# Early q, k and v loads over 128 partitions, 64x64 turns of q and k, a layer norm without a reciprocal, and a new order

## The chip, the cores and the metric

One core of one Trainium2 chip runs the whole kernel. The metric is the device time of one execution in microseconds. The core's engines are named as the profile names them: PE (matrix products, with PEld for its weight loads), DVE (vector), ACT (scalar), POOL (GpSimd) and SP, which only issues transfers. Every transfer of this kernel is issued by SP, in program order, into one queue that is served by the core's 16 DMA engines.

## The reference, cut to what matters

```python
# q, k, v: (8 batches, 8 heads, 576 positions, 64), float32
q_d, k_d, v_d = means over groups of 4 positions          # 144 pooled positions
out_d  = softmax(q_d @ k_d.T / 8) @ v_d                   # dense attention on the pooled rows
out_up = repeat(out_d, 4 positions)
scores = where(|i - j| < 4, q @ k.T / 8, -1e9)            # a band of 7 positions
x      = out_up + softmax(scores) @ v                     # 4608 tokens x 512
h      = x @ w_in                                         # 512 -> 1024 (weights arrive as float64)
solu   = h * softmax(h)
ln     = (solu - mean(solu)) / sqrt(var(solu) + 1e-6) * g_ln
out    = ln @ w_out                                       # 1024 -> 512
```

## The kernel before

The work has two halves that run interleaved. **Attention** goes batch by batch (8 of them). For a batch, q and k are loaded in four pairs of heads, turned so that the head dimension lies on partitions (`qT`, `kT`), and summed over groups of four into `qd` and `kd`. The pooled part (`Pooled`, two groups of pairs) makes scores `sd`, the softmax `pd`, its transpose `pdt`/`pdT` and the product `po` with the pooled values `vd`. The local part works on windows of 64 positions: scores `sc`, softmax `pl`, transpose `plt`/`plT`, and the product `xp` with `vw`, another load of v. Both are added into `x`. **The feed-forward half** goes tile by tile, 36 tiles of 128 tokens: `xhl` splits x into a high and a low part, `ffn_in` makes `h` with 24 matmuls of 128x512, then the softmax, `e`, the mean and the variance; `e` is written to memory as `u` and read back as `v` in another layout (`ffn_back`), transposed by 32x32 blocks on DVE, split into `uh` and `ul`, and multiplied by `w_out` in `ffn_out` (`o`, again 24 matmuls), whose result is scaled by `s` on its way out.

At the start the 16 pieces of the two weight matrices are loaded as float64 (512 KB each, tiles `stage` and `w_2` ... `w_15`) and turned into high and low float32 parts, mostly on DVE. Batches 0 and 1 are "early" (`EARLY = 2`): their q and k are loaded in rows and turned on PE against the identity (`qp`, `kp`); later batches are turned on DVE.

`load_vs` loads the values for the pooled sum, three tiles `vs_0` to `vs_2` for each batch, each with four positions side by side in a row of 256 elements. `pooled_vsum` adds them into `vd` (lines L466 and L469 of before, on POOL or DVE). All three must be summed before `po`.

Nothing here is ordered by the hardware's choice: `plan` is a list of steps, the table `ORDER` says in what order the steps are written, and `OTHER` names the steps that go to their second choice of engine. Each engine then runs its own instructions strictly in that order. SP's transfers have eight semaphores in turn (DMAHW0 to DMAHW7), and an issue waits until the one eight before it has landed, so at most eight are in flight.

Of the kernel before, what the change touches and what calls it, by code (L numbers as in the profile page):

```python
# [10 lines left out]
F32 = mybir.dt.float32  # L11
# [117 lines left out]
def pooled_local_attention_then_solu_ffn(  # L129
# [343 lines left out]
    class EarlyBatch(Batch):  # L473

        TT = 6
        TP = S // TT

        def room(self):  # L480
# [625 lines left out]
```

## Time and profile before

| | |
|---|---|
| time, median of 3 runs | 596.7 us (593.45 to 599.17) |
| the profiled execution | 600.77 us, of which the span is 599.0 us |
| mean granted PE clock | 0.975 |
| PE busy | 562.0 us, 94% |
| DVE / ACT / POOL busy | 469.1 / 331.6 / 297.0 us |
| transfers | 101.27 MB, mean 169 GB/s |
| chain that ended last | PE 52%, DVE 16%, SP's queue 10%, DMA 8% |

The page's busy shares are means over a start of some 120 us, in which weights are unpacked and two batches are prepared, a long middle in which attention and the feed-forward tiles alternate on PE, and a short end. The stretches have to be read one by one. A row of the timeline or of a group gives start, busy time, line, engine, operation, output<-input and count.

### The profile page before, as it was taken

To read this page: it belongs to the slowest core of one execution; us is meant where nothing else is said; L and a number is where in the kernel's file an instruction comes from. 1 tells how busy PE (TensorE), PEld (TensorE's weight loads), DVE (VectorE), ACT (ScalarE), POOL (GpSimd) and SP (SyncE) were. 2 spreads that over 40 slices of the span, in tenths; PEclk is the share of its full clock that TensorE was granted. 3 is DMA by queue.
4 is the path that set the end of the run, shared out by engine and by line. 5 is a ranking of instruction groups with operands and counts; after the bars stand their busy time and mean duration, and the time that the engine had idled before them with its cause. 6 is when DMAs were issued, how large, how long until landed. Compare 5 with 4: busy or idle time off the path is not lost.

```text
span 599.0 us, 16898 instructions
## 1 busy us (share of the span) xinstructions
PE 562.0 (94%) x6748; PEld 440.0 (73%) x6748; DVE 469.1 (78%) x712; ACT 331.6 (55%) x692; POOL 297.0 (50%) x444
## 2 busy tenths in 40 slices
PE   7896989899997999999979999999999999999997
PEld 2664757677786778878757778778878788788875
DVE  3989899999986888888868898896898678554551
ACT  2766668655864666536437554547645464443542
POOL 2367388764177464575634446453554464432320
PEclk9989799899997999999999999999999999999999
DMA  8998878579778778776788775678453746133421
GB/s 228 250 202 210 200 154 189 137 180 226 175 160 197 184 181 205 196 139 171 178 182 206 199 229 144 134 164 245 144 142 122 202 119 216 39 106 106 140 89 71
DMA packets 209039, 101.27 MB, mean 169 GB/s; under 512 B 163520, under 2 KB 195264, under 8 KB 208960
## 3 DMA queue, kind: packets, MB, share of 16 engines
q1 hardware_dynamic: 208960, 100.19, 66.4%
q8 instruction: 53, 0.87, 0.6%
q14 instruction: 26, 0.21, 0.1%
HBM read 67.11 MB, written 27.79 MB: 158 GB/s over the span
## 4 chain that ended last, share of the span: by engine, by line
PE 52%; DVE 16%; SPq 10%; DMA 8%; issue 5%; POOL 4%; ACT 2%; DVEq 0%; POOLq 0%; ACTq 0%
PE o L945 21%; PE h L822 20%; SPq L262 4%; DMA v<-u 3%; SPq L693 3%; SPq L897 2%; DMA qm<-in_q_dram 2%; PE warm L1002 2%; PE po L804 2%; DMA stage<-in_moe_w_in_dram 2%; DVE st L831 2%; DVE e L836 2%; DVE w L357 1%; POOL ul L928 1%; PE sd L743 1%
## 5 line engine op out<-in xcount | busy, mean ns | idle before, releaser
L822 PE MATMUL h<-wi_h,xh 128*128 128x512 f32 x288 | 116.5, 405 | 5.5 <-DVE e L836 5.4
L945 PE MATMUL o<-wo_h,uh 128*128 128x512 f32 x288 | 118.0, 410 | 1.0 <-ACT osb L952 0.8
L822 PE MATMUL h<-wi_h,xl 128*128 128x512 f32 x288 | 114.7, 398 | 0.0
L822 PE MATMUL h<-wi_l,xh 128*128 128x512 f32 x288 | 114.7, 398 | 0.0
L945 PE MATMUL o<-wo_l,uh 128*128 128x512 f32 x288 | 113.7, 395 | 0.0
L945 PE MATMUL o<-wo_h,ul 128*128 128x512 f32 x288 | 79.0, 396 | 1.4 <-DVE ul L928 1.4
L822 PEld LDWEIGHTS h<-wi_h,xh 128*128 128x128 f32 x288 | 54.8, 190 | 20.0 <-DVE e L836 4.1
L834 ACT ACTIVATE e<-h,st 128x1024 f32<-128x1024 f32 x36 | 40.1, 1115 | 51.8 <-DVE st L831 50.7
L831 DVE TENSOR_REDUCE st<-h 128x1 f32<-128x1024 f32 x36 | 43.9, 1218 | 29.0 <-PE h L822 27.4
L945 PEld LDWEIGHTS o<-wo_h,uh 128*128 128x128 f32 x288 | 54.3, 189 | 16.6 <-ACT osb L952 2.1
L928 POOL TENSOR_TENSOR ul<-v,uh 128x512 fp32r<-128x512 f32 x39 | 51.3, 1320 | 28.8 <-ACT uh L925 27.3
L945 PEld LDWEIGHTS o<-wo_h,ul 128*128 128x128 f32 x288 | 53.9, 188 | 15.1 <-DVE ul L928 2.2
L925 ACT ACTIVATE uh<-v 128x512 fp32r<-128x512 f32 x70 | 43.2, 625 | 39.2 <-DVE v L918 25.6
L822 PEld LDWEIGHTS h<-wi_h,xl 128*128 128x128 f32 x288 | 54.7, 190 | 13.4 <-POOL xl L979 0.2
L918 DVE STREAM_TRANSPOSE v<-v 128x512 f32<-128x512 f32 x70 | 47.1, 692 | 21.8 <-DMA v<-u 21.2
L822 PEld LDWEIGHTS h<-wi_l,xh 128*128 128x128 f32 x288 | 54.8, 190 | 12.5
L945 PEld LDWEIGHTS o<-wo_l,uh 128*128 128x128 f32 x288 | 54.3, 189 | 11.2
L840 POOL TENSOR_SCALAR st<-st 128x1 f32<-128x1 f32 x36 | 8.8, 244 | 102.3 <-DVE e L836 95.5
L836 DVE SCALAR_TENSOR_TENSOR e<-h,e 128x1024 f32<-128x1024 f32 x36 | 43.7, 1213 | 13.9 <-ACT e L834 13.8
L874 ACT ACTIVATE e<-e 128x1024 f32<-128x1024 f32 x35 | 36.7, 1050 | 16.1 <-DMA u<-e 11.9
L979 POOL TENSOR_TENSOR xl<-x,xh 128x512 fp32r<-128x512 f32 (+1 forms) x29 | 33.7, 1166 | 20.2 <-ACT xh L976 19.9
L952 ACT ACTIVATE osb<-o,s 128x512 f32<-128x512 f32 x36 | 24.4, 678 | 23.1 <-PE o L945 14.5
(127 smaller groups left out, 1099.3 us busy)
## 6 DMA issues: line engine op xcount, KB each, us to landing
u<-e SPq DMA_DIRECT2D x35, 512.0 KB, 3.2
v<-u SPq DMA_DIRECT2D x140, 128.0 KB, 3.3
out_dram<-osb SPq DMA_DIRECT2D x36, 256.0 KB, 3.1
qm<-in_q_dram SPq DMA_DIRECT2D x96, 72.0 KB, 3.3
km<-in_k_dram SPq DMA_DIRECT2D x96, 72.0 KB, 2.4
vs<-in_v_dram SPq DMA_DIRECT2D x24, 256.0 KB, 4.1
vw<-in_v_dram SPq DMA_DIRECT2D x80, 64.0 KB, 3.0
vw<-in_v_dram SPq DMA_DIRECT2D x40, 128.0 KB, 3.4
```

The lines of the kernel that those rows point to most:

```text
L262: nc.sync.dma_start(t[nm][Q * 32:Q * 32 + 32, pr], src[b, 2 * pr + par, :, dh * 32:dh * 32 + 32].rearrange("(k t) d -> t k d", t=32),)
L822: nc.tensor.matmul(hps[:, n, :], src[:, cc, :], wt[:, cc, n * 512:(n + 1) * 512], start=(cc == 0 and src is xh and wt is wi_h), stop=(cc = ...
L831: nc.vector.tensor_reduce(out=nmx, in_=hf, op=ALU.max, axis=AX.X, negate=True)
L834: nc.scalar.activation(e, hf, AF.Exp, bias=nmx, scale=1.0, accum_out=se)
L836: nc.vector.scalar_tensor_tensor(out=e, in0=hf, scalar=1.0, in1=e, op0=ALU.mult, op1=ALU.mult, accum_out=su)
L874: nc.scalar.activation(e0, e, AF.Square, accum_out=m2)
L918: nc.vector.transpose(vg, vg)
L925: nc.scalar.activation(uh, tp, AF.Copy)
L928: (usual if v is None else engine(usual, nc.vector)).tensor_tensor(out=ul, in0=tp, in1=uh.bitcast(F32), op=ALU.subtract)
L945: nc.tensor.matmul(o, src[:, j, :], wt[:, 4 * g + j, :], start=(g == 0 and j == 0 and src is uh and wt is wo_h), stop=(g == 1 and j == 3 a ...
L952: nc.scalar.activation(osb, o, AF.Copy, scale=s)
L979: engine(nc.gpsimd, nc.vector).tensor_tensor(out=l, in0=src, in1=h.bitcast(F32), op=ALU.subtract)
```

## The change

1. **q and k of batches 0 and 1.** A pair of heads was loaded as 96 partitions x 2 heads x 384 elements; it is now 128 partitions x 576 elements, one contiguous run of 2,304 bytes on each. The turn on PE was 12 products of 96x64 by 96x96 for each tensor and pair; it is now 18 products of 64x64 by 64x64.
2. **vs of batches 0 and 1.** A tile was two issues of 64 and 48 partitions x 4 heads x 256 elements; it is now four issues (one for each of four heads `h`) of 128 partitions x 256 elements. The source of each is written as 2 halves x 64 rows x 256 elements. 448 KB a tile become 512 KB.
3. **Layer norm.** The factor was r = 1/se, va = r*r*m2/DFF + 1e-6, s = va^-0.5 * r. It is now s = (m2/DFF + 1e-6*se*se)^-0.5, with se*se*1e-6 made on POOL right behind se. For each tile a DVE reciprocal and two of seven small POOL instructions go.
4. **A new order** of the same steps, and a new list of steps that use their other engine.

```diff
 ORDER = """
-18 21 4 11 23 8 32 22 12 142 143 33 158 34 7 15 159 144 160 145 146 147 148 149 150 151 152 153
...
+9 1 3 4 150 151 152 153 154 155 7 10 2 32 34 142 33 24 158 25 143 156 35 157 36 37 159 26 38 27
...
     def load_vs(b, c):
         vs = big(f"vs_{b}_{c}").rearrange("p (h x) -> p h x", h=H // 2)
-        for half, n in ((0, 64), (1, KN)):
-            src = v[b, half * (H // 2), c * KN * FAC, :]
-            nc.sync.dma_start(
-                vs[half * 64:half * 64 + n],
-                bass.AP(
-                    tensor=src.tensor, offset=src.offset,
-                    ap=[[FAC * D, n], [S * D, H // 2], [1, FAC * D]],
-                ),
-            )
+
+        def source(head, dims):
+            at = v[b, head, c * KN * FAC, :]
+            return bass.AP(tensor=at.tensor, offset=at.offset, ap=[*dims, [1, FAC * D]])
+
+        if b < EARLY:
+            for h in range(H // 2):
+                nc.sync.dma_start(vs[:, h], source(h, [[H // 2 * S * D, 2], [FAC * D, 64]]))
+        else:
+            for half, n in ((0, 64), (1, KN)):
+                nc.sync.dma_start(
+                    vs[half * 64:half * 64 + n],
+                    source(half * (H // 2), [[FAC * D, n], [S * D, H // 2]]),
+                )
         return vs[0:ROOM]
...
         def load_one(self, pr, nm):
-            src = {"q": q, "k": k}[nm]
-            if pr == 3:
-                self.qk[nm, pr] = big(f"{nm}m_{self.b}_3")[:, 0:self.TT * 2 * D]
-            t = self.qk[nm, pr][0:self.TP].rearrange("p (par x) -> p par x", par=2)
-            self.qk[nm, pr] = t.rearrange("p par (t d) -> p par t d", t=self.TT)
             nc.sync.dma_start(
-                t, src[self.b, 2 * pr:2 * pr + 2].rearrange("h (p t) d -> p h (t d)", t=self.TT)
+                self.qk[nm][:, pr * S:(pr + 1) * S],
+                {"q": q, "k": k}[nm][self.b, 2 * pr:2 * pr + 2].rearrange(
+                    "h (p t) d -> (h p) (t d)", t=self.TT
+                ),
             )
...
                 for t in range(self.TT):
-                    at = t % HT * self.TP
                     for par in range(2):
                         nc.tensor.matmul(
-                            tp[rows(par), t // HT, at:at + self.TP],
-                            self.qk[nm, pr][:, par, t],
-                            ident[0:self.TP, 0:self.TP], start=True, stop=True,
+                            tp[rows(par), t], src[rows(par), t], ident[rows(par), rows(par)],
+                            start=True, stop=True,
                         )
...
+        nc.gpsimd.tensor_scalar(
+            out=se, in0=se, scalar1=se, scalar2=1e-6, op0=ALU.mult, op1=ALU.mult
+        )
...
-        nc.vector.reciprocal(out=r, in_=se)
-        yield
-        nc.gpsimd.tensor_tensor(out=va, in0=r, in1=r, op=ALU.mult)
-        yield
         nc.scalar.activation(e0, e, AF.Square, accum_out=m2)
         yield
-        nc.gpsimd.tensor_tensor(out=va, in0=va, in1=m2, op=ALU.mult)
         nc.gpsimd.tensor_scalar(
-            out=va, in0=va, scalar1=1.0 / DFF, scalar2=1e-6, op0=ALU.mult, op1=ALU.add
+            out=m2, in0=m2, scalar1=1.0 / DFF, scalar2=se, op0=ALU.mult, op1=ALU.add
         )
-        nc.gpsimd.tensor_tensor(out=va, in0=va, in1=mhalf, op=ALU.pow)
-        nc.gpsimd.tensor_tensor(out=s, in0=va, in1=r, op=ALU.mult)
+        nc.gpsimd.tensor_tensor(out=s, in0=m2, in1=mhalf, op=ALU.pow)
```

What the order makes of it is seen best in the engines' own sequences. **SP, where the first values are loaded.** In these rows `qm` and `km` are q and k (the numbered names mark the batch's buffer), `vw` and `vs` the two loads of v, `stage` and `w_N` weight pieces; the sizes are partitions x runs x elements. Before, from batch 1's first k load:

```order
L495 DMA km_390<-in_k_dram 96x2x384
L495 DMA km_3_404<-in_k_dram 96x2x384
L495 DMA km_390<-in_k_dram 96x2x384
L337 DMA stage<-in_moe_w_in_dram 128x1024
L495 DMA km_390<-in_k_dram 96x2x384
L294 DMA vs_0_409<-in_v_dram 64x4x256
L294 DMA vs_0_409<-in_v_dram 48x4x256
L495 DMA qm_3_412<-in_q_dram 96x2x384
L294 DMA vs_1_414<-in_v_dram 64x4x256
L294 DMA vs_1_414<-in_v_dram 48x4x256
```

The same place of SP's sequence in the changed kernel, from the first vs issue to the last k load of batch 1:

```order
L294 DMA vs_0_369<-in_v_dram 128x1x256 x4
L486 DMA qm_364<-in_q_dram 128x576 x2
L486 DMA km_365<-in_k_dram 128x576
L337 DMA w_9_419<-in_moe_w_out_dram 128x1024
L486 DMA km_365<-in_k_dram 128x576
L294 DMA vs_1_422<-in_v_dram 128x1x256 x4
L337 DMA stage<-in_moe_w_in_dram 128x1024
L276 DMA vw_0_428<-in_v_dram 64x4x64 x4
L486 DMA km_365<-in_k_dram 128x576
L324 DMA g_sb<-in_moe_g_ln_dram 128x8x1
L294 DMA vs_2_436<-in_v_dram 128x1x256 x4
L486 DMA qm_364<-in_q_dram 128x576
```

All three vs tiles, twelve issues, now stand ahead of batch 1's last q and k loads; before, all of batch 1's k loads stood ahead of them. (The row behind the last one shown is the last k load, `km_365`.)

**PE, up to the first product with the pooled values.** The name `kp_1_3` is the turn of k for batch 1, pair 3; `po_0_0` is batch 0's first product with `vd`. Before:

```order
L510 MATMUL kp_1_1_737<-ident_82,km_1_390 64x96 x12
L743 MATMUL sd_1_0_762<-kd_1_652,qd_flat_115 64x144 x12
L607 MATMUL plt_0_1_783<-ident_82,pl_1_108 128x128 x4
L510 MATMUL kp_1_3_788<-ident_82,km_1_3_404 64x96 x12
...
L785 MATMUL pdt_0_1_860<-ident_82,pd_0_1_606 48x48 x36
L804 MATMUL po_0_0_900<-pdT_0_0_701,vd_0_730 64x144 x12
```

and in the changed kernel:

```order
L503 MATMUL qp_1_3_838<-ident_82,qm_1_364 64x64 x18
L734 MATMUL sd_1_0_859<-kd_1_823,qd_flat_115 64x144 x12
L503 MATMUL kp_1_3_877<-ident_82,km_1_365 64x64 x18
...
L776 MATMUL pdt_0_1_954<-ident_82,pd_0_1_737 48x48 x36
L795 MATMUL po_0_0_992<-pdT_0_0_817,vd_0_819 64x144 x12
```

The left-out rows are products on constants (`warm`). In both kernels `kp_1_3` stands ahead of `po_0_0`; its load is now the last of that part of SP's sequence.

**SP, where batch 1's values are loaded.** `u` is a tile written to memory, `v` the same tile read back. Before:

```order
L868 DMA u_1445<-e_1289 128x1024
L281 DMA vw_2_1447<-in_v_dram 64x4x64 x4
L294 DMA vs_2_1637<-in_v_dram 64x4x256
L294 DMA vs_2_1637<-in_v_dram 48x4x256
L281 DMA vw_4_1675<-in_v_dram 64x4x64 x4
L294 DMA vs_1_1692<-in_v_dram 64x4x256
L294 DMA vs_1_1692<-in_v_dram 48x4x256
L897 DMA v_1695<-u_1445 32x4x256 x4
```

and in the changed kernel:

```order
L863 DMA u_1654<-e_1423 128x1024
L276 DMA vw_1_1656<-in_v_dram 64x4x64 x4
L294 DMA vs_2_1661<-in_v_dram 128x1x256 x4
L886 DMA v_1666<-u_1654 32x4x256 x4
L294 DMA vs_1_1671<-in_v_dram 128x1x256 x4
L863 DMA u_1955<-e_1579 128x1024
```

Tile 1's read back now stands between the two vs tiles instead of behind both. Further on, the order on PE is nearly that of before: the `h` and `o` groups follow each other in the same turn, with a few attention steps moved by one place.

More of the change, by code (lines that the diff above doesn't have):

```diff
@@ L473, in pooled_local_attention_then_solu_ffn @@
     class EarlyBatch(Batch):
-        TT = 6
-        TP = S // TT
+        TT = S // 64
         def room(self):
-            qk = {}
-            n = self.TT * 2 * D
-            for nm in ("q", "k"):
-                t = load.tile([P, NPR * S], F32, tag=f"{nm}m", name=f"{nm}m_{self.b}")
-                for pr in range(3):
-                    qk[nm, pr] = t[:, pr * n:(pr + 1) * n]
-            return qk
-        def load_one(self, pr, nm):
-            src = {"q": q, "k": k}[nm]
-            if pr == 3:
-                self.qk[nm, pr] = big(f"{nm}m_{self.b}_3")[:, 0:self.TT * 2 * D]
-            t = self.qk[nm, pr][0:self.TP].rearrange("p (par x) -> p par x", par=2)
-            self.qk[nm, pr] = t.rearrange("p par (t d) -> p par t d", t=self.TT)
+            return {
+                nm: load.tile([P, NPR * S], F32, tag=f"{nm}m", name=f"{nm}m_{self.b}")
+                for nm in ("q", "k")
+            }
+        def load_one(self, pr, nm):
             nc.sync.dma_start(
-                t, src[self.b, 2 * pr:2 * pr + 2].rearrange("h (p t) d -> p h (t d)", t=self.TT)
+                self.qk[nm][:, pr * S:(pr + 1) * S],
+                {"q": q, "k": k}[nm][self.b, 2 * pr:2 * pr + 2].rearrange(
+                    "h (p t) d -> (h p) (t d)", t=self.TT
+                ),
             )
         def pair_steps(self, pr):
-            HT = self.TT // 2
-            n = HT * self.TP
             for nm, dst in (("q", self.qT[:, pr]), ("k", self.kT[:, pr])):
@@ L506, in pair_steps @@
                     tp = two_banks(ps_a, "a", f"{nm}p_{self.b}_{pr}")
+                tp = tp.rearrange("p a n -> p (a n)")[:, 0:S].rearrange("p (t n) -> p t n", t=self.TT)
+                src = self.qk[nm][:, pr * S:(pr + 1) * S].rearrange("p (t d) -> p t d", t=self.TT)
                 for t in range(self.TT):
-                    at = t % HT * self.TP
                     for par in range(2):
                         nc.tensor.matmul(
-                            tp[rows(par), t // HT, at:at + self.TP],
-                            self.qk[nm, pr][:, par, t],
-                            ident[0:self.TP, 0:self.TP], start=True, stop=True,
+                            tp[rows(par), t], src[rows(par), t], ident[rows(par), rows(par)],
+                            start=True, stop=True,
                         )
@@ L517, in pair_steps @@
                     engine(nc.scalar, nc.vector),
-                    dst.rearrange("x (p a t) -> x p a t", a=2, t=HT),
-                    tp[:, :, 0:n].rearrange("x a (t p) -> x p a t", t=HT),
+                    dst.rearrange("x (p t) -> x p t", t=self.TT), tp.rearrange("x t p -> x p t"),
                 )
@@ L828, in ffn_in @@
         hf = hps.rearrange("p a n -> p (a n)")
-        stat = small.tile([P, 7], F32, tag="st", name=f"st_{i}", bufs=3)
-        nmx, se, su, nmu, r, va, m2 = (stat[:, n:n + 1] for n in range(7))
+        stat = small.tile([P, 5], F32, tag="st", name=f"st_{i}", bufs=3)
+        nmx, se, su, nmu, m2 = (stat[:, n:n + 1] for n in range(5))
         nc.vector.tensor_reduce(out=nmx, in_=hf, op=ALU.max, axis=AX.X, negate=True)
@@ L1012, in tile_in @@
         row(xhl(i), 2)
-        row(ffn_in(i), 12 if i not in ON_PE else 11)
+        row(ffn_in(i), 10 if i not in ON_PE else 9)
         if i not in ON_PE:
```

181 rows, old and new, of tables (ORDER, OTHER) are left out of this document.

## The prediction

> **What bounds the kernel now.** I read the table of stretches first, because the page's shares are means over unlike stages. Four of its rows (from:to, length, busy time and instruction count of PE, PEld, DVE, ACT and POOL, then granted clock, share of DMA time, GB/s):
>
> ```profile
> 0.00:20.00 20.00, 16.17 (x190) 9.39 (x190) 10.67 (x24) 8.12 (x13) 4.05 (x12) 1.00 0.90 240
> 20.00:60.00 40.00, 30.52 (x660) 20.80 (x656) 36.99 (x59) 26.10 (x72) 25.19 (x21) 0.96 0.94 213
> 60.00:120.00 60.00, 53.30 (x936) 41.52 (x940) 55.48 (x91) 43.62 (x79) 42.20 (x42) 0.89 0.74 170
> 120.00:571.00 451.00, 438.42 (x4879) 349.75 (x4871) 358.02 (x530) 243.71 (x513) 222.02 (x358) 0.99 0.66 167
> ```
>
> From 120 to 571 us PE is busy 438.42 of 451 us, so a faster neighbour there is worth at most the 12.6 us that PE still idles. The first 120 us differ: the DMA engines are nearly full (shares 0.90 and 0.94), and DVE is busy 36.99 of 40 and 55.48 of 60 us. Which of the two comes last, the chain that ended last tells (start, length, what):
>
> ```profile
> 17.18 1.00 PE qp L510 x24
> ...
> 19.55 11.36 DMA qm<-in_q_dram
> ...
> 31.34 9.91 DMA stage<-in_moe_w_in_dram
> ...
> 46.59 2.87 DVE w L361
> ...
> 57.94 1.01 PE po L804 x24
> ```
>
> Turns of q and k on PE carry it up to 18.2 us, two transfers from 19.55 to 41.25 us, then mostly DVE's weight work, until PE's first product with the pooled values, `po`, at 57.94 us. The start is bound by the queue of loads, then by DVE. Since PE's order is fixed, what comes late in the start moves nearly everything behind it.
>
> **The change part by part.** The sum is made against the profiled execution: 600.77 us, 1.8 us of it outside the span of 599.0. The median shown is 596.7, so the result is multiplied by 596.7/600.77 = 0.993 at the end.
>
> *Turns of q and k.* A float32 product is two instructions. The trace has no turn of 64x64, but the scores are products of exactly that shape:
>
> ```profile
> 53.49 1.21 PE L510 MATMUL kp<-ident,km 96*64 96x96 f32 x24
> 23.91 0.69 PE L560 MATMUL sc<-kT,qT 64*64 64x64 f32 x32
> ```
>
> 12 products (24 instructions) take 1.21 us; 18 of 64x64 (36 instructions) should take 36/32 of 0.69, or 0.78 us. 16 turns save 6.9 us of PE. PE idles 9.5 us between 20 and 60, waiting for others, so most of that is hidden; the five turns on the chain between 11 and 18.2 us save 5 x 0.4 = **2 us**, if their loads are there (the end on the other side is 0).
>
> *Layer norm.* Rows of one instruction: minimum/median/maximum in ns.
>
> ```profile
> L870 DVE RECIPROCAL st<-st x36: 111/150/164, 93.4 to 581.0; 128x1 f32<-128x1 f32 x36
> L872 POOL TENSOR_TENSOR st<-st x36: 183/195/672, 93.7 to 581.3; 128x1 f32<-128x1 f32 x36
> L876 POOL TENSOR_TENSOR st<-st x36: 183/195/747, 95.5 to 585.4; 128x1 f32<-128x1 f32 x36
> ```
>
> 36 x 0.150 = 5.4 us of DVE and two POOL instructions, 36 x 0.39 = 14 us of POOL, go. They make `s`, wanted only when `o` is finished, and 32 of the 36 tiles lie where PE is the bound. In the start DVE sheds 4 x 0.15 us. I take **-1 us**, between 0 and the 12.6 us of PE idling; what hides the rest is PE's own work. The new order of the middle is near the old one group by group; I give it 0, with the same lower end and some 5 us of harm as the upper one.
>
> *Loads of q and k.* They are the same bytes, 288 KB an issue, in fuller rows. By bytes they cost the same in a queue that is full: **0**. The end of gain is below, with the rivals.
>
> *Loads of vs.* This is the large term. The issues of before, with KB each and median us from issue to landing:
>
> ```profile
> vs<-in_v_dram SPq DMA_DIRECT2D x24, 256.0 KB, 4.1
> plT<-pl SPq DMA_DIRECT2D x80, 64.0 KB, 2.4
> vs<-in_v_dram SPq DMA_DIRECT2D x24, 192.0 KB, 4.5
> km<-in_k_dram SPq DMA_DIRECT2D x8, 288.0 KB, 10.7
> ```
>
> Every issue of before has the same slowest count on both its sides, and that count (128, 96, 64, 48 or 32) is a multiple of 16. A new vs issue has 128 partitions on one side and a slowest count of 2 on the other. The trace doesn't show how such a one is spread, so I bound it: at best over all 16 DMA engines as every other, at worst over two, one for each half of the source. Landing times above don't follow bytes alone (192 KB after 4.5 us, 256 KB after 4.1), so shape does count, though queueing is in those numbers too. I take **two engines**, the only cut that both sides have in common at their slowest level, and keep both ends.
>
> The Trainium skill, DMA: Bandwidth & Descriptors, section "Why a DMA increments its semaphore by 16 and not by 1", has a rule for this: a transfer runs on the largest number of engines, at most 16, that divides the slowest count above one of both sides, and on the lowest-numbered ones. By that rule every new vs issue goes to the same two engines and the sum stands as below; by the landing rows, read as full width for all issues, it would be the first rival's. No run here shows it yet.
>
> What two engines give is a rate for each engine. GB/s divided by 16 and by the share of DMA time gives 240/(16 x 0.90) = 16.7 and 213/(16 x 0.94) = 14.2 in the crowded start, and in emptier stretches
>
> ```profile
> 500.00:550.00 50.00, 50.00 (x472) 40.03 (x471) 31.53 (x49) 22.79 (x49) 18.76 (x39) 1.00 0.32 103
> 571.00:599.00 28.00, 23.57 (x105) 18.55 (x103) 7.90 (x13) 10.02 (x16) 3.60 (x14) 0.96 0.24 85
> ```
>
> 20.1 and 22.1. With two engines working and fourteen waiting, the emptier rows are the nearer: I take 20, with 16 and 22 as ends.
>
> Now the first batch. On each engine a 512 KB load puts 32 KB, a 288 KB load 18, the four issues of a vw 16, and a vs tile on its two engines 256 KB. The 13 loads ahead of batch 1's first q load (5 of weights, 8 of q and k) are 4.98 MB; at 240 GB/s they are in at 20.8 us. From that q load to batch 1's last k load the changed order has 18+32 (a q, w_3), 256 (vs_0), 36+18+32+18 (two q, k, w_9, k), 256 (vs_1), 32+16+18 (stage, vw_0, k), 256 (vs_2), 18+18 (q, k): 1024 KB, 1.05 MB, on each of the two engines. At 20 GB/s that takes 52.4 us, with 2.4 us to land (the row of plT): 75.6 us. That last k load is what `kp_1_3` turns, and PE stands there until it is in; SP can't go around it, with eight issues in flight at most. Before:
>
> ```profile
> 57.94 0.97 PE L804 MATMUL po<-pdT,vd 48*64 48x144 f32 x24 [0.84 <-ACT pd L762]
> ```
>
> `kp_1_3` started at 53.49 and `po` 4.45 us later. So `po` comes at 80.1 instead of 57.94: **+22 us** (+17 at 22 GB/s, +35 at 16). Behind PE, DVE and ACT wait for `kp` and `xp`, and the later weight pieces wait in the same queue, so nothing is done ahead meanwhile. SP itself issues 12 more vs loads; an issue takes a median of 607 ns:
>
> ```profile
> L294 SPq DMA_DIRECT2D vs<-in_v_dram x48: 312/607/2693, 33.5 to 469.5; - x48
> ```
>
> 7.3 us of SP, hidden here under its waits for landings (without that cover, 3.6 us a batch).
>
> *The second batch.* Its vs_0 goes out while the first tiles run, and is wanted late. vs_2 and vs_1 stand behind the write of `u` for tile 1:
>
> ```profile
> 99.41 0.55 SPq L868 DMA_DIRECT2D u<-e  x1
> 123.42 0.84 PE L804 MATMUL po<-pdT,vd 48*64 48x144 f32 x20
> L466 POOL TENSOR_TENSOR vs<-vs x19: 1261/1291/1737, 44.9 to 509.6; 112x512 f32<-112x512 f32 x19
> L469 POOL TENSOR_TENSOR vd<-vs x19: 727/745/1072, 46.3 to 511.0; 112x256 f32<-112x256 f32 x19
> ```
>
> From that write to batch 1's `po` there were 24.0 us. Now two engines carry 32+16+256+32+256 = 592 KB (0.606 MB) in between: 30.3 us at 20 GB/s, plus 2.4 to land and 2.0 of sums on POOL, 34.7 us. That is 10.7 us too late; at 22 GB/s 8, at 16 GB/s 18; 0 if the writes of `u` come earlier or DVE, at 55.48 of 60 us, is later anyway. I take **+8 us**. Tile 1's read back waits behind vs_2 too, inside the same time.
>
> **The sum:** 600.8 + 22 + 8 - 2 - 1 = 627.8 us, times 0.993: **623 us**. Its ends: 600.8 + 17 + 0 - 10 = 608, or 604; and 600.8 + 35 + 18 + 0 = 654, or 649.
>
> **The rivals.**
>
> *Full width, and faster (0.32 in all).* If the vs issues use all engines, or successive ones use different ones, a tile is 32 KB on an engine, the same stretch holds 352 KB (0.36 MB), and at 14.2 GB/s it is in 25.4 us after 20.8, with landing 48.6: ahead of the 53.49 at which `kp_1_3` stood before. DVE's work then sets `po` as before, and only the -2 and -1 remain: 597.8, or 594 us (0.20). If fuller rows also lift the crowded queue from 213 to the first stretch's 240 GB/s, its 8.5 MB between 20 and 60 us take 35.5 instead of 40 us, and with half of the 12.6 us of later idling the gain is 2 + 4.5 + 6 = 12.5: 588.3, or 584 us (0.12). It decides at the landing of batch 1's last k load: before 53.5 us this rival holds, after it mine. For it speaks that all landing rows of before are within a few us; against it, that none of them has unequal sides.
>
> *Two engines, but covered (0.06).* The 1.05 MB would have to be in by 53.5 - 2.4, or 30.3 us after 20.8: 34.6 GB/s on one engine, and no row gives more than 22.1. What is left to it is that PE has slack ahead of `kp_1_3` and later; 600 us.
>
> **How the numbers follow.** Forecast 0.62, full width 0.32, covered 0.06. A change of about 1% is what can be told from none here: 591 to 603. The forecast's case is slower throughout (604 to 649). Of full width, 584 is faster and 594 mostly the same, with 0.06 of its 0.20 below 591. Covered is the same but for 0.01. Faster 0.18, same 0.19, slower 0.63. The range leaves out the lower part of full width (0.13) and the last 0.05 above: 589 to 647.
>
> **What would show it.** If I am right, the new vs issues land after 10 us and more instead of 4.1, DMA share and GB/s fall between 25 and 75 us, `kp_1_3` waits for its load, and `po` starts near 80 us; from batch 1's `po` on, tiles follow at the old pace, with PE as busy as before. The turns should take 0.8 us, and POOL's busy time should fall by some 14 us. I am wrong if the vs issues land as fast as the others, or if the stall is there but PE makes it up: then `po` is late and the end isn't.

## The result, and the profile after

The changed kernel takes 634.65 us (median of 4, 632.39 to 637.53) against 597.62 us before: a ratio of 1.063, 95% interval 1.056 to 1.071. The forecast was 623 us, between 589 and 647. Its profiled execution took 636.78 us, of which the span is 635.0.

The same four stretches, then two short ones, of the changed kernel (from:to, length, busy time and count of PE, PEld, DVE, ACT and POOL, granted clock, DMA share, GB/s):

```profile
0.00:20.00 20.00, 15.01 (x302) 10.12 (x302) 13.27 (x26) 9.06 (x15) 5.26 (x13) 1.00 0.69 251
20.00:60.00 40.00, 25.50 (x544) 18.36 (x540) 26.05 (x47) 19.14 (x51) 14.67 (x12) 0.87 0.40 126
60.00:120.00 60.00, 49.09 (x760) 38.58 (x761) 46.67 (x79) 37.95 (x80) 38.96 (x38) 0.83 0.69 175
120.00:571.00 451.00, 419.19 (x5082) 332.69 (x5081) 341.70 (x484) 248.72 (x517) 210.04 (x275) 0.96 0.67 166
26.00:30.00 4.00, 3.83 (x76) 1.93 (x72) 4.00 (x9) 2.52 (x5) 2.50 (x2) 1.00 0.14 48
147.00:150.00 3.00, 0.47 (x8) 0.01 (x3) 0.00 (x0) 2.45 (x5) 0.00 (x0) 0.50 0.14 47
```

From 20 to 60 us the DMA share fell from 0.94 to 0.40 and the rate from 213 to 126 GB/s, just where the load queue had been the bound. In the two short stretches the transfers of a row of vs issues are under way: a share of 0.14 of 16 engines is 2.2 engines, and they move 47 to 48 GB/s. Successive issues don't spread further, since the share stays at 0.14 with several in flight: they share the same engines.

The chain that ended last, up to the first `po` (start, length, what):

```profile
36.08 3.23 SPq L294
39.35 11.12 DMA vs<-in_v_dram
...
53.66 3.69 SPq L294
57.40 8.70 DMA qm<-in_q_dram
...
66.23 2.08 PE qp L503 x34
...
74.67 0.80 PE po L795 x22
```

Before, the chain ran here over DVE's weight work. Now SP stands at the vs issues, a vs transfer takes 11 us, and batch 1's last q load, issued behind them, takes 8.7 us. `po` began at 74.46 us, 16.5 later than before, and the first tile of the feed-forward half is as late (84.38 against 67.91).

PE's timeline at batch 1's first product with the pooled values, and the issues of the early values (start, busy time, engine, line, operation, count; then a line's minimum/median/maximum in ns):

```profile
146.71 0.76 PE L795 MATMUL po<-pdT,vd 48*64 48x144 f32 x8 [7.55 <-DVE pl L569]
157.27 1.24 PE L795 MATMUL po<-pdT,vd 48*64 48x144 f32 x16 [9.80 <-DVE vd L469]
```

```profile
L294 SPq DMA_DIRECT2D vs<-in_v_dram x24: 527/1520/3690, 20.1 to 145.4; - x24
```

PE waits 7.55 and then 9.80 us; the rest of `po` runs at 157.27 instead of 123.42 us, +33.9. The first wait hangs on tile 1's read back, which stands behind vs_2 in SP's sequence (DVE waits 9.36 us for it), the second on vs_1. From there the distance nearly stays: batch 7's first `po` stands at 554.63 against 518.39, +36.2, and the span is 36.0 us longer. So most of the loss arises before 165 us, in two steps, +16.5 at the first `po` and +17.4 more up to batch 1's. Some of it is the clock, which the forecast didn't price and whose share was not measured: from 157 to 160 us the granted clock is 0.50, and a product of `o` takes 0.63 us where it takes 0.39 to 0.40 from 165 us on.

### The profile page after: what moved, and what is told of

Read it like the earlier page. It is cut to its first block, busy times and chain, and to the rows that moved or that the text cites. A ratio compares the mean times of both kernels' runs of the same rounds, so it can differ in the third digit from the quotient of the medians.

```text
span 635.0 us, 17193 instructions
## 1 busy us (share of the span) xinstructions
PE 569.0 (90%) x6940; PEld 447.6 (70%) x6940; DVE 455.6 (72%) x673; ACT 339.0 (53%) x702; POOL 282.8 (45%) x365
## 4 chain that ended last, share of the span: by engine, by line
PE 56%; SPq 15%; DMA 11%; DVE 9%; issue 3%; POOL 3%; ACT 3%; DVEq 0%; ACTq 0%; POOLq 0%
PE o L934 24%; PE h L813 20%; DMA vs<-in_v_dram 5%; SPq L257 4%; SPq L294 4%; SPq L886 2%; SPq L276 2%; PE po L795 2%; PE xp L696 2%; PE warm L991 2%; DMA v<-u 2%; PE sd L734 1%; PE pdt L776 1%; DMA qm<-in_q_dram 1%; SPq L270 1%
## 5 line engine op out<-in xcount | busy, mean ns | idle before, releaser
L934 PE MATMUL o<-wo_l,uh 128*128 128x512 f32 x288 | 115.8, 402 | 0.0
L917 POOL TENSOR_TENSOR ul<-v,uh 128x512 fp32r<-128x512 f32 x39 | 51.5, 1321 | 79.1 <-ACT uh L914 67.7
L907 DVE STREAM_TRANSPOSE v<-v 128x512 f32<-128x512 f32 x70 | 47.1, 691 | 27.2 <-DMA v<-u 27.2
L831 POOL TENSOR_SCALAR st<-st 128x1 f32<-128x1 f32 x36 | 11.9, 331 | 101.0 <-DVE e L827 100.7
L853 ACT ACTIVATE e<-e,st 128x1024 f32<-128x1024 f32 x27 | 30.9, 1145 | 14.1 <-POOL st L831 12.4
```

Of the source, the lines that this page charges most:

```text
L853: nc.scalar.activation(e, e, AF.Identity, bias=nmu, scale=1.0)
L907: nc.vector.transpose(vg, vg)
L917: (usual if v is None else engine(usual, nc.vector)).tensor_tensor(out=ul, in0=tp, in1=uh.bitcast(F32), op=ALU.subtract)
L934: nc.tensor.matmul(o, src[:, j, :], wt[:, 4 * g + j, :], start=(g == 0 and j == 0 and src is uh and wt is wo_h), stop=(g == 1 and j == 3 a ...
```

## The experiments

Times are medians; each ratio is to the kernel before, run beside it on the same chip.

**1. The changed kernel with the values loaded as before.**

```diff
-        if b < EARLY:
+        if b < 0:
```

> The changed kernel with the early values loaded as before (two issues a tile, of 64 and 48 partitions x 4 heads x 256); the new order, the q and k loads, the turns and the layer norm stay as changed. Two-engine theory: both stalls go, so the first pooled product `po` starts at 55 to 60 us instead of 74.5 and batch 1's no longer waits for a vs load; 634.65 less 16.5 and 19 is about 599, less what the other parts are worth, so 593 to 600 us, a ratio of 0.99 to 1.005 to the kernel before. Rival, the new order itself (or the fuller q and k rows) is what costs: 620 us or more, with `po` still past 70 us.

Measured: 596.81 us, ratio 0.999 (0.995 to 1.003), `po` at 52.1 us, earlier than expected. The whole loss is in the vs loads; the order, the q and k loads, the turns and the layer norm come to nothing together.

**2. The kernel before with the changed vs loads alone.** Its `load_vs` is replaced by that of the changed kernel.

> The kernel before with only the early values loaded as in the changed kernel (four issues a tile, 128 partitions x 256, source 2 x 64 rows). Two-engine theory: a tile needs 256 KB on each of two engines, 11.7 us at the 22.3 GB/s that one engine shows; three tiles from 33.5 us on land at about 70 instead of 47, so `po` comes at 70 to 75 us (+12 to +17), and batch 1's vs_2 and vs_1, 23.5 us from 103.5 us on and 2 us of sums, make its `po` come 6 to 15 us later still: 615 to 630 us. Rival, the new order is what costs: 596 to 601 us, a ratio of 1.00.

Measured: 639.5 us, ratio 1.072 (1.066 to 1.078), above the 615 to 630 that had been expected. The order is cleared from this side too. The last part of the first `po` ran at 73.7 us, as expected, but batch 1's came at 158.9 us, 35.5 late where up to 32 had been expected: the second stall is larger than I thought.

**3 and 4. The 128-partition loads for one batch alone.**

```diff
-        if b < EARLY:
+        if b < 1:       # and, in the other kernel, b == 1
```

> The changed kernel with the 128-partition value loads for batch 0 alone; batch 1 loads its values in the two issues of before. Two-engine theory: two separate stalls, the first (+16.5 us to the first `po`) stays and the second (+19 us up to batch 1's `po`) goes: 634.65 - 19 = 616, so 611 to 620 us. Rival, one delay that grows (the late first batch itself makes the second late): 628 us or more. Rival, the stalls hide each other: under 606 us.

> The changed kernel with the 128-partition value loads for batch 1 alone; batch 0 loads its values in the two issues of before. If the two stalls are separate and add up, this is 634.65 less what batch 0's loads cost (616.85 - 596.81 = 20.0 for batch 1 repaired against both repaired): 613 to 618 us, with the first `po` at 52 us as in the kernel with both repaired. If a later start hides part of the second stall or lengthens it, the two single costs don't add up to the 37.8 us of both: under 610 or over 621 us.

Measured: 616.85 us for batch 0 alone, 1.034 (1.028 to 1.039), and 615.76 us for batch 1 alone, 1.035 (1.029 to 1.041). Against the 596.81 us of experiment 1 that is 20.0 and 19.0 us, together 39.0; both at once cost 37.8. The stalls are separate and nearly add up.

**5. Eight issues a tile, full width.**

```diff
             for h in range(H // 2):
-                nc.sync.dma_start(vs[:, h], source(h, [[H // 2 * S * D, 2], [FAC * D, 64]]))
+                for half in range(2):
+                    nc.sync.dma_start(
+                        vs[half * 64:half * 64 + 64, h], source(half * (H // 2) + h, [[FAC * D, 64]])
+                    )
```

> The changed kernel with each of the four early issues of a values tile cut in two, of 64 partitions x 256 each: the same bytes (512 KB a tile) and the same rows, but eight issues a tile, whose slowest count is 64 on both sides. Two-engine theory: all sixteen engines, each issue costs SP some 0.6 us (4.8 us a tile, where the changed kernel's four took 7 to 9 us): 594 to 603 us. Rival, what costs is the number of issues, at 1.5 us of SP each: 24 more of them add up to 36 us, 640 us or more. Rival, what costs is the 128th to 64th extra bytes (64 KB a tile): no change from 634.

Measured: 611.17 us, 1.023 (1.017 to 1.030). Missed: above the first theory and far below the other two. The issues took the 0.6 us that I had expected, but eight of them are 5.0 to 6.9 us of SP's time a tile, and SP had no room for it: the chain between 35 and 60 us is nearly SP alone, issue behind issue.

```profile
42.73 0.60 SPq L295
43.37 1.28 SPq L295
44.70 0.60 SPq L295
45.35 0.58 SPq L489
45.98 0.43 SPq L489
46.45 0.63 SPq L276
```

(L295 is vs, L489 q and k, L276 vw.) The first `po` was at 57.0 us, 5 later than in experiment 1. The larger part of the loss comes behind it: the last part of batch 1's `po` ran at 127.80 against 114.53 us, 13.3 later.

**6. Four issues a tile, full width.** Same number of issues and bytes as the changed kernel; only the shape of an issue differs.

```diff
-            for h in range(H // 2):
-                nc.sync.dma_start(vs[:, h], source(h, [[H // 2 * S * D, 2], [FAC * D, 64]]))
+            for h in (0, 2):
+                for half in range(2):
+                    nc.sync.dma_start(
+                        vs[half * 64:half * 64 + 64, h:h + 2],
+                        source(half * (H // 2) + h, [[FAC * D, 64], [S * D, 2]]),
+                    )
```

> The changed kernel with the same four issues a values tile and the same 512 KB, but each issue of 64 partitions x 2 heads x 256 elements (slowest count 64 on both sides) instead of 128 partitions with a source of 2 x 64 rows. Only the spread over the engines differs from the changed kernel. Two-engine theory: nearly all of the loss goes; between the 596.8 us of two issues a tile and the 611.2 of eight, so 599 to 604 us, an issue taking about 0.6 us of SP. Rival, four issues and 64 KB more a tile are what costs, by SP's time: 625 us or more, with issues of 1.5 us.

Measured: 595.9 us, 0.9975 (0.9945 to 1.0004), `po` at 51.5 us; that is below the 599 to 604 expected, so the twelve issues more than in experiment 1 cost nothing. This is the clean comparison: 38.75 us for the shape of 24 issues. Its issues, and the stretch from 26 to 30 us that stood above with 0.14 and 48 GB/s:

```profile
L295 SPq DMA_DIRECT2D vs<-in_v_dram x24: 601/606/1547, 19.4 to 109.7; - x24
```

```profile
26.00:30.00 4.00, 3.83 (x56) 1.65 (x45) 4.00 (x8) 2.89 (x5) 2.87 (x2) 1.00 1.02 351
```

**7. Is it the unequal sides, or the count?** The kernel before, with 64 partitions cut into 62 and 2; both sides of every issue are alike.

```diff
-        for half, n in ((0, 64), (1, KN)):
+        for p0, half, row0, n in ((0, 0, 0, 62), (62, 0, 62, 2), (64, 1, 0, KN)) if b < EARLY else ((0, 0, 0, 64), (64, 1, 0, KN)):
...
```

> The kernel before with the first early issue of each values tile, 64 partitions x 4 heads, cut into 62 and 2 partitions; the other stays at 48 partitions. The bytes stay, both sides have equal counts everywhere, and there are three issues instead of two. Theory that the slowest counts set the number of engines: 62 is divided by 2 and by no larger number up to 16, so 248 packets a tile go to two engines, 124 on each, 5.7 us a tile instead of the 11.7 of the changed loads, and SP stands at these issues for 2 us and more: 608 to 625 us, about half of what the changed loads cost this kernel (+41). Rival, only two unequal sides are cut to two engines: one issue more a tile at 0.6 us, 597 to 602 us, with all issues near 0.6 us.

Measured: 614.97 us, 1.028 (1.022 to 1.034). An ordinary-looking cut into 62 and 2 partitions costs nearly half of what the changed loads cost this kernel (17.6 of 41 us). So the sides need not differ; the count decides. One line of its issues, all shapes together, and a stretch with the third tile's 62 partitions under way:

```profile
L294 SPq DMA_DIRECT2D vs<-in_v_dram x54: 253/602/6295, 31.3 to 486.2; - x54
```

```profile
48.00:52.00 4.00, 3.89 (x28) 1.74 (x28) 3.61 (x7) 1.00 (x3) 0.44 (x1) 0.57 0.14 40
```

The share is 0.14 again. The longest issue, 6.3 us, is one of 2 partitions and 8 KB (at 38.61 us) right behind one of 62: SP stands at it for about the 6 us that the 248 KB ahead of it take at the 40 GB/s of this stretch. Two engines for such a load is as the Trainium skill has it, DMA: Bandwidth & Descriptors, section "Why a DMA increments its semaphore by 16 and not by 1": the largest number up to 16 that divides the slowest counts, which for 62 is 2. The traces agree, for 62 partitions here and for the 2 x 64 rows above (0.14 of 16 engines each).

**8. The same issues from ACT's queue.**

```diff
-                nc.sync.dma_start(vs[:, h], source(h, [[H // 2 * S * D, 2], [FAC * D, 64]]))
+                nc.scalar.dma_start(vs[:, h], source(h, [[H // 2 * S * D, 2], [FAC * D, 64]]))
```

> The changed kernel with the 24 early value issues, unchanged in shape, given out by ACT instead of SP, at the same places of the program; so they keep to two engines but no longer hold SP. Theory that most of the loss is SP standing at these issues, with the other loads behind it: q and k of batch 1 come early again, and what is left is the tiles' own landing (three tiles, 35 us of transfer from 20 us on, so `po` at 60 to 66 us) and ACT's own standing: 605 to 622 us. Rival, the loss is the two engines' own work, whoever issues: `po` at 72 us or later, 628 to 640 us. Above 640 us: ACT held by these issues costs more than SP held.

Measured: 652.15 us, 1.091 (1.086 to 1.097); `po` at 86.0 us: the last case expected, above 640 us. The loss went with the issues. SP gave out batch 1's last q and k loads by 37 us instead of 60, but ACT stood; SP in its turn waited 18.1 us at a vw issue for a vs load to land, since the eight semaphores in turn count ACT's issues too. ACT's timeline:

```profile
31.84 25.33 ACTq L294 DMA_DIRECT2D vs<-in_v_dram  x8
57.22 0.21 ACT L749 ACTIVATE pd<-pd 128x6 f32<-128x6 f32 x1 [24.74 <-DMA vs<-in_v_dram]
```

Eight issues hold it 25.3 us, 3.2 us each: 128 KB in that time is 41 GB/s. After the first few, an issue lasts about as long as the two engines take to move one. This run doesn't split the changed kernel's loss into SP standing and tiles landing, since the ACT work behind the issues (the softmax of `pd`) is on the path itself; that division stays open.

**9 and 10. The small terms.** The kernel before with the new layer norm alone, and with it and the new q and k loads and turns.

```diff
-        nc.vector.reciprocal(out=r, in_=se)
...
-        nc.gpsimd.tensor_tensor(out=s, in0=va, in1=r, op=ALU.mult)
+        nc.gpsimd.tensor_tensor(out=s, in0=m2, in1=mhalf, op=ALU.pow)
```

> The kernel before with the layer norm of the changed kernel and nothing else; the steps that lose their instruction stay in the order, empty. The forecast gave it 1 us, between 0 and 12.6: 594 to 598 us, a ratio of 0.997 to 1.000. Both parts of this and the q and k loads together measured 1.0039 [1.0009, 1.007]: if the layer norm is what costs there, 599 to 601 us here; if it is the q and k loads, or the gain of one eaten by the other, under 598.

> The kernel before, its order and its value loads, with the changed q and k loads and turns and the changed layer norm. By the forecast's terms these are worth 2 and 1 us: 0.993 to 0.997 of before, 594 to 597 us. Rival, the fuller q and k rows also lift the crowded load queue (the changed kernel with the old value loads moved 255 and 230 GB/s in the first two stretches, against 240 and 213): `po` some 5 us earlier than 57.9 and 588 to 593 us. If the earlier `po` of that run (52.1) came from the new order instead, `po` stays at 55 us or later here.

Measured: 598.25 us, 1.003 (0.999 to 1.006), and 599.45 us, 1.004 (1.001 to 1.007). Neither brings its microsecond, and the pair costs perhaps 2. The first `po` stands at 54.9 in the run with the layer norm alone, whose changed instructions begin only at 75.5 us, and at 55.0 with the q and k loads: two executions differ by 3 us there with nothing changed ahead of it, so a gain of that size at `po` can't be put down to the q and k loads.

**11 and 12. The best version, and its layer norm.** Experiment 6 with more rounds, and the same with the layer norm of before.

```diff
+        nc.vector.reciprocal(out=r, in_=se)
+        nc.gpsimd.tensor_tensor(out=va, in0=r, in1=r, op=ALU.mult)
         nc.scalar.activation(e0, e, AF.Square, accum_out=m2)
...
```

> The changed kernel with full-width value loads in four issues of 64 partitions x 2 heads, again, with more rounds: the only version so far whose median lies under the kernel before (0.9975, 0.9945 to 1.0004). If the new order with the fuller q and k rows is worth a little, 593 to 597 us and an interval that ends under 1.000; if the first reading was chance, 0.998 to 1.003.

> The same with the layer norm of before put back (reciprocal and r*r in the step ahead of the square). Alone on the kernel before, the new layer norm measured 1.0027 (0.999 to 1.0064). If it costs there by what it does, and not by chance, this is 1 to 2 us below the kernel beside it; if it is worth the 1 us of the forecast, 1 us above; within 1 us either way says that the term is too small to see.

Measured: 596.34 us, 0.999 (0.996 to 1.001), so no gain that can be told from none; and 602.42 us, 1.010 (1.007 to 1.012). Placed so in the new order, the old layer norm costs 6 us; in the old order it cost nothing. In that run POOL's longest wait in total was for the reciprocal, which I put in another step than before, so this says what a wait of POOL on DVE at that place costs, and not what the arithmetic costs:

```profile
POOL st L867 <- DVE st L866: 81.5, 27, 7.5
```

(The columns are us in total, times, longest.) No version beats the kernel before clearly.

## Why the prediction was right, point by point

- **Two engines for a vs issue: right**, shown by the shares of 0.14, by experiment 6 (only the shape of the issues differs, 38.75 us) and by experiment 7.
- **The rate of an engine: a little too low.** 48 GB/s on two is 24 each by the bytes; 20 was taken and 22 was the upper end. With 24 the forecast's own sum puts the first `po` at 71.4 us instead of 80.1.
- **First batch, +22: the mechanism right, the size in part by luck.** PE stood for batch 1's last loads as forecast, though for the last q load, one issue ahead of the k load that was named. `po` came at 74.5 instead of the 80.1 that was worked out, +16.5 against the 57.9 of before. But in the new order with full-width loads it comes at 51.5 (experiment 6): both ends of the difference were some 6 us too late, and the difference, 22.9, came out. By time, with all else of the change in place, batch 0's loads cost 20.0 us.
- **Second batch, +8: too small, and this is the step that failed.** It costs 19.0 us alone and 17.8 on top of the first; 18 was the upper end. Two things were wrong in it. The first is the base of the difference. The stretch from the write of `u` to `po` was well worked out (32.9 us against 34.7):

```profile
124.42 0.44 SPq L863 DMA_DIRECT2D u<-e  x1
```

But I subtracted from it the 24.0 us of before, and those belong to the old order. In the old order the difference holds: in experiment 2 the stretch is 34.0 us, 10.0 longer, though tile 1's read back came last there and not the values. In the new order it takes 15.8 us when the loads are of full width. Experiment 6, its write and its `po`:

```profile
98.88 0.44 SPq L867 DMA_DIRECT2D u<-e  x1
114.71 1.20 PE L799 MATMUL po<-pdT,vd 48*64 48x144 f32 x24
```

So the stretch is 17 us longer, not 10.7; what makes it shorter in the new order to begin with was not traced. The second thing is batch 1's vs_0, which I priced at nothing because it is wanted late: it holds SP, and with it all loads behind. SP's timeline of the changed kernel, then of experiment 6:

```profile
75.71 6.72 SPq L294 DMA_DIRECT2D vs<-in_v_dram  x4
```

```profile
55.22 2.55 SPq L295 DMA_DIRECT2D vs<-in_v_dram  x4
```

The way from the first `po` to that write, which the forecast gave no term, is longer by 6.0 us with batch 1's loads narrow alone (53.0 in experiment 4 against 47.1 in experiment 1) and by 4.2 on top of batch 0's (50.0 against 45.8 in experiment 3). With both, batch 1's `po` is some 23 us later in either comparison, of which 18 to 19 are left at the end; where the rest is made up was not traced.

- **An issue at 607 ns, 7.3 us more for SP, hidden: half right.** For full-width issues it is so (606 ns, and experiment 6 loses nothing by its twelve more); for two-engine issues the median is 1,520 ns. The price of these instructions was taken from issues of another shape.
- **Turns of 64x64, -2: wrong.** I took the rate of `sc`. All the turns' busy time on PE, before and after:

```profile
L510 PE MATMUL qp<-ident,qm 96*64 96x96 f32 x192 | 10.1, 256 | 3.1 <-DMA qm<-in_q_dram 2.0 <-ACT pd L762 0.8 <-ACT qT L239 0.3
L510 PE MATMUL kp<-ident,km 96*64 96x96 f32 x192 | 9.6, 249 | 0.0
```

```profile
L503 PE MATMUL kp<-ident,km 64*64 64x64 f32 x288 | 12.3, 247 | 12.6 <-DMA km<-in_k_dram 6.1 <-ACT qT L234 5.2 <-issue 1.3
L503 PE MATMUL qp<-ident,qm 64*64 64x64 f32 x288 | 10.6, 230 | 8.1 <-DMA qm<-in_q_dram 8.1
```

(Behind the first bar stand the busy time of all in us and the mean of one in ns; single ones overlap.) The busy time rose from 19.7 to 22.9 us where a fall by 6.9 was expected. Part of these turns ran in the stall, at a granted clock of 0.50 (66 to 70 us); without the stall, in experiment 6, all of them take 19.8 us, as much as before. An instruction then takes 34 ns instead of 51, but there are half as many again; the rate taken from `sc`, 0.69 us for 32, is 22.
- **Layer norm, -1:** nothing can be seen of it (experiment 9). POOL's busy time fell by 14 us, from 297.0 to 282.8, but that this is the 14 that was forecast is luck: the new layer norm alone took off 5.0 (292.0 in experiment 9), and some 6 us went with three of the 19 pairs of vs sums on POOL, which the new list gives to DVE. What covers the small gain was not tried.
- **Full width, the rival: right about what would follow from it.** With full-width loads the kernel stands at 596 to 597 us; 594 was worked out. Its test decided as it should: batch 1's last q load lands at 66.1 us, well behind the 53.5 that was named.

The sum, +27 us, missed the measured +37 by about the second batch's 10; the range held, since its upper end had 18 for this batch.

## What to carry to other kernels

Look at the slowest count (the number of rows in the outermost dimension) of both sides of a load before its bytes and its rows: loads with a slowest count of 2, or of 62, cost 18 to 41 us here, and the same bytes as the former in four issues of 64 partitions cost nothing. A narrow transfer also holds the queue that issues it, so price it by what stands behind it there, and moving it to another queue moved the loss here. When a stretch of before is the base of a difference and the order changes too, ask how long that stretch is in the new order: here it was 15.8 us and not 24.0.

## What was not expected of the hardware

An issue to two engines isn't a constant 0.6 us for the issuing queue: in a row of them it lasts, after the first two or three, about as long as the transfer of one (2.7 us for 128 KB at 48 GB/s): 3.2 us on ACT and up to 3.7 on SP. Full-width issues kept to 0.6 us, but as a sum they have an edge: twelve more of them were free, thirty-six more cost 14 us (596.81 to 611.17).
